# Mixture-of-experts kernel: the token lists by 9 wide products instead of 36 narrow ones, and low parts ahead of the routing's search

## The chip, the cores and the metric

The kernel runs on one core of one Trainium2 chip. The metric is the device time of one execution in microseconds (us). Engines: PE is TensorE, DVE VectorE, ACT ScalarE, POOL GpSimd, SP SyncE (which issues most DMAs).

## The reference

Pooled attention gives 4608 tokens of 512 features; the tokens then go to 8 experts of 576 tokens each. Logits of all tokens and experts are taken in descending order, and each token goes to the first expert of its own that still has room. Each expert is two matrix products with a ReLU between.

```python
logits = x @ w_gate                       # x: [4608, 512], 8 experts
order = np.argsort(-logits.flatten())
for idx in order:
    tok, e = int(idx) // E, int(idx) % E
    if assigned[tok] >= 0 or counts[e] >= cap:   # cap = 576
        continue
    assigned[tok] = e
    counts[e] += 1
for e in range(E):
    mask = assigned == e
    out[mask] = np.maximum(x[mask] @ w1[e], 0.0) @ w2[e]   # w1 512x1024, w2 1024x512
```

## The kernel before

**Attention** (to about 137 us) works on 36 tiles of 128 tokens, writes the tokens to `xd` in DRAM and keeps their logits in `lg`, 36 columns of 8 on 128 partitions.

**Routing** has 8 phases; each finds the next expert that fills up and the list of its tokens. A phase is a Python generator (`phase`, `search`, `close`), and its yields are the steps that a planner places. First the best remaining expert of each token (`best`), then four rounds of search for the threshold. A round compares (`cmp`, L598), counts by 9 products (L641, into `diagc` and `cnt`), sums by a fold (L652), tests (`g`, L659), and spreads the answer (L666). The first phase's rounds use narrow products (L603). `close` then makes the list: `own` marks the tokens, a scan and two products (L700, L701) number them (`si`), and each number is split into a low part of 5 bits and a block. `OHa` is a one-hot of the low part (L718), `OHb` a one-hot of the block times the token's column (L712) and, by ACT, times its partition (L713). 36 products, one for each column (L724), add both up: four groups of 32 partitions of PSUM for the columns modulo four, with 40 values. `cp` copies them out (L726), 8 products with `spread` (L732) bring the four groups together, and `rows` (L735) are the 576 token numbers as 5 columns of 128. Two products more (L750 and the counts around it) close the books. The step that yields "id" starts the DMA of the expert's w1, "rows" the gathers.

**Experts.** For each, POOL gathers the tokens' rows by five indirect DMAs (`xg`, L972); PE transposes each tile (L1004) into one of two PSUM banks `tp`; ACT copies out a rounded high part `xh`, and DVE takes the low part `xl`, what is left (L1008), which frees the bank. Weights are split likewise: `w1h` by ACT (L980), `w1l` by DVE (L984), eight pieces an expert; `w2h`, `w2l` (L990, L993). Stage 1 (L1028) adds three products of high and low parts, in blocks of 12 matmuls with 256 or 320 tokens; ACT writes `hh` and DVE the low part `hl` (L1036). Stage 2 (L1062, and L1067 for the last 64 rows) gives the output, which POOL scatters. The transposes of the next expert stand in stage 2, the last two sets in the next stage 1. The first expert takes w1 in two halves; a copy `late` (L1257), put behind an `xl` on DVE, makes the address of the second half, and another that of w2.

**What sets the order.** The order is written out as the program is built. Each engine does its list in order. `experts` keeps an estimated time `now`, moved by each PE matmul; `later` queues DVE work that is to be issued when its input should be there; `step` issues one step of the routing and estimates from its two numbers when DVE will be done (`ready`, `dve`). `advance` first issues queued work that is due, and then a routing step, unless its turn has not come. Between those, `Pieces` puts in parts of the weights. The line that decides is

```python
elif ready > now or waiting and turned[0] < 5 or not step(e):
```

so that the search goes ahead whenever its own last step should be done; only the first expert's transposes (`turned[0] < 5`) hold it, as long as anything is queued.

## Time and profile before

| | us |
|---|---|
| median of 3 runs | 629.12 |
| lowest, highest | 628.36, 630.3 |
| the profiled execution | 630.56 |
| its span, first to last instruction | 628.8 |
| mean granted TensorE clock | 0.986 |

In the profile a row of a view in order of time gives start, length, engine, line, operation, output<-inputs, shapes and count; in brackets stands how long the engine was idle before it and what released it. Rows of one line that follow each other are merged. Ends of matmuls are modelled and overlap, so the distance of starts is what one costs. A row of groups gives after the first bar the busy us and the mean ns of one, after the second the idle time before them.

### The profile page before, as it was taken

The page shows a single profiled execution, that of the slowest core. Times are in us where ns is not written, and L with a number is a line of the kernel's source. Part 1 is how long each engine was busy: PE and PEld are TensorE (multiplying, and loading weights), DVE is VectorE, ACT ScalarE, POOL GpSimd, SP SyncE. Part 2 cuts the span into 40 slices and gives each one's busy share as a digit, 9 for nine tenths or more (in the row PEclk, how much of TensorE's full clock was granted, in tenths as well). Part 3 has the DMA queues.
Part 4 walks back from the last instruction along what each step waited for, and adds up shares of the span by engine and source line. Part 5 has one row for each costly group of instructions (what it writes and reads, how often), then busy time and mean ns, then how long its engine had stood idle before and what let it go on. Part 6 is the DMA issues. An engine that isn't in the chain of part 4 may idle for free.

```text
span 628.8 us, 11882 instructions
## 1 busy us (share of the span) xinstructions
PE 602.0 (96%) x4543; PEld 521.4 (83%) x4543; DVE 391.4 (62%) x1142; ACT 242.9 (39%) x562; POOL 176.6 (28%) x218
## 2 busy tenths in 40 slices
PE   8999999985899999999999999999999999999994
PEld 6899999873797689769978987897799889879972
DVE  7587777887884778767862785386468326505300
ACT  7444444452451335233541433253336325514310
POOL 2999998001101410323011302120230113020021
PEclk9999999995999999999999999999999999999998
DMA  8999952222432543319003701640180046014011
GB/s 352 418 422 398 425 213 75 82 85 97 143 125 95 165 159 135 93 52 329 24 34 103 284 1 50 213 158 17 51 324 28 34 161 225 18 47 149 2 40 41
DMA packets 32611, 92.21 MB, mean 147 GB/s; under 512 B 3472, under 2 KB 3472, under 8 KB 29856
## 3 DMA queue, kind: packets, MB, share of 16 engines
q1 hardware_dynamic: 21296, 62.92, 26.7%
q0 software_dynamic: 5920, 18.95, 8.6%
q10 hardware_dynamic: 5328, 9.48, 4.0%
q8 instruction: 38, 0.62, 0.4%
q14 instruction: 29, 0.24, 0.1%
HBM read 72.46 MB, written 18.87 MB: 145 GB/s over the span
## 4 chain that ended last, share of the span: by engine, by line
PE 79%; issue 7%; DVE 5%; DMA 4%; POOL 3%; SPq 1%; ACT 1%; POOLq 0%; another core or an unknown queue 0%; ACTq 0%
PE h L1028 29%; PE h L1062 23%; PE psa L269 7%; PE pss L227 5%; PE h L1067 4%; PE tp L1004 2%; DMA rawk<-in_k_dram 2%; PE pse L256 2%; PE rt L256 1%; PE rt L724 1%; PE rt L641 1%; PE rt L217 1%; PE rt L603 1%; DMA out_dram<-yt,rows 1%; DMA raw<-in_moe_w_dram 1%
## 5 line engine op out<-in xcount | busy, mean ns | idle before, releaser
L1042 POOL DMA_INDIRECT out_dram<-yt,rows x29 | 30.6, 1056 | 264.3 <-ACT yt L1076 264.1
L1062 PE MATMUL h<-w2h,hl 128*128 128x512 f32 x256 | 102.6, 401 | 0.0
L1062 PE MATMUL h<-w2l,hh 128*128 128x512 f32 x256 | 102.0, 398 | 0.0
L1062 PE MATMUL h<-w2h,hh 128*128 128x512 f32 x256 | 101.1, 395 | 0.3 <-PEq L1126 0.3
L1028 PE MATMUL h<-xl,w1h 128*128 128x320 f32 (+1 forms) x512 | 95.1, 301 | 0.2 <-DVE late L1257 0.2
L1028 PE MATMUL h<-xh,w1l 128*128 128x320 f32 (+1 forms) x512 | 92.1, 298 | 0.5 <-DVE g L659 0.5
L1028 PE MATMUL h<-xh,w1h 128*128 128x320 f32 (+1 forms) x512 | 91.9, 300 | 0.3 <-issue 0.3
L1033 ACT ACTIVATE hh<-h 128x320 fp32r<-128x320 f32 (+1 forms) x128 | 52.0, 410 | 101.0 <-PE h L1028 97.9
L1028 PEld LDWEIGHTS h<-xh,w1h 128*128 128x128 f32 x512 | 75.6, 189 | 3.1 <-issue 3.1
L1028 PEld LDWEIGHTS h<-xl,w1h 128*128 128x128 f32 x512 | 76.8, 190 | 1.1 <-DVE late L1257 0.4
L1028 PEld LDWEIGHTS h<-xh,w1l 128*128 128x128 f32 x512 | 75.9, 189 | 0.9 <-DVE w1l L984 0.6
L972 POOL DMA_INDIRECT xg<-xd,rows x40 | 39.8, 995 | 125.4 <-DVE rows L735 69.1
L1008 DVE TENSOR_TENSOR xl<-tp,xh 128x512 fp32r<-128x512 f32 (+1 forms) x40 | 25.3, 633 | 78.4 <-ACT xh L1006 77.8
L1036 DVE SCALAR_TENSOR_TENSOR hl<-h,hh 128x320 fp32r<-128x320 f32 (+1 forms) x128 | 57.1, 451 | 26.6 <-ACT hr L1035 14.5
L1076 ACT ACTIVATE yt<-h 128x512 f32<-128x512 f32 x32 | 19.1, 597 | 123.8 <-PE h L1062 103.4
L269 PE MATMUL psa<-vblk,eT 128*128 128x146 f32 (+3 forms) x400 | 62.0, 302 | 0.0
L1062 PEld LDWEIGHTS h<-w2h,hh 128*128 128x128 f32 x256 | 48.2, 188 | 9.2 <-issue 0.7
L1062 PEld LDWEIGHTS h<-w2h,hl 128*128 128x128 f32 x256 | 48.3, 189 | 8.7
L1062 PEld LDWEIGHTS h<-w2l,hh 128*128 128x128 f32 x256 | 48.4, 189 | 8.2
L269 PEld LDWEIGHTS psa<-vblk,eT 128*128 128x128 f32 (+1 forms) x400 | 52.2, 180 | 1.7 <-POOL tk L172 0.3
L993 DVE TENSOR_TENSOR w2l<-raw,w2h 128x512 fp32r<-128x512 f32 x64 | 43.2, 681 | 3.7 <-ACT w2h L990 3.6
L984 DVE TENSOR_TENSOR w1l<-raw,w1h 128x512 fp32r<-128x512 f32 x64 | 41.2, 684 | 6.8 <-ACT w1h L980 6.4
(210 smaller groups left out, 907.9 us busy)
## 6 DMA issues: line engine op xcount, KB each, us to landing
raw<-in_moe_w_dram SPq DMA_DIRECT2D x64, 512.0 KB, 6.5
xd<-xt ACTq DMA_DIRECT2D x36, 256.0 KB, 3.9
rawv<-in_v_dram SPq DMA_DIRECT2D x7, 1280.0 KB, 8.4
rawk<-in_k_dram SPq DMA_DIRECT2D x7, 1152.0 KB, 11.6
rawq<-in_q_dram SPq DMA_DIRECT2D x7, 1152.0 KB, 13.3
rawk<-in_k_dram SPq DMA_DIRECT2D x2, 576.0 KB
rawv<-in_v_dram SPq DMA_DIRECT2D x1, 768.0 KB, 8.2
rawq<-in_q_dram SPq DMA_DIRECT2D x1, 640.0 KB, 9.1
```

Source lines behind the costliest of these rows:

```text
L227: nc.tensor.matmul(ps[cols, j // 2, 144 * (j % 2):144 * (j % 2) + 144], self.q_of(b, j, n, cols.stop - cols.start), self.kblk[b % 4][:, j] ...
L269: self.nc.tensor.matmul(o[h], self.eT[i][:, c, h], self.vblk[b % 4][:, self.BLOCKS[c]:self.BLOCKS[c + 1]], start=(c == cs[0]), stop=(c == ...
L972: nc.gpsimd.indirect_dma_start(out=self.xg[:n, t, :], out_offset=None, in_=self.xd, in_offset=bass.IndirectOffsetOnAxis(ap=rows[:n, t:t + ...
L984: self.nc.vector.tensor_tensor(l, raw, h.bitcast(F32), op=OP.subtract)
L993: self.nc.vector.tensor_tensor(self.w2l[:, i], self.raw2[e][:, i], self.w2h[:, i].bitcast(F32), op=OP.subtract)
L1008: later(1.3, 0.65, lambda: nc.vector.tensor_tensor(xl, ps[:, :, :n], xh, op=OP.subtract))
L1028: nc.tensor.matmul(ps[:, :m], a[:, j, fs], b[:, j, o], start=(n == 0), stop=(n == 11))
L1033: nc.scalar.activation(hh[:, f, o], ps[:, :m], AF.Relu)
L1036: later(0.65, 0.4, lambda f=f, o=o, m=m, ps=ps: nc.vector.scalar_tensor_tensor(hl[:, f, o], ps[:, :m], 0.0, hh[:, f, o].bitcast(F32), op0= ...
L1042: st = nc.gpsimd.indirect_dma_start(out=rows, out_offset=bass.IndirectOffsetOnAxis(ap=idx, axis=0), in_=y, in_offset=None)
L1062: nc.tensor.matmul(ps, a[:, f, o], b[:, f], start=(f == 0 and k == 0), stop=(f == 7 and k == 2))
L1067: nc.tensor.matmul(ps[64 * a:64 * a + 64, :256], self.hr[:, f], self.raw2[e][:, f, 256 * a:256 * a + 256], start=(f == 0), stop=(f == 7))
```

## The change

The list's 36 products become 9. Columns are regrouped so that product b holds the four columns b, b+9, b+18, b+27; the weights are 32 low parts times four columns, 128 in all, the moving side 20 blocks times four columns, 80. Of the 128x80 result only the entries count whose two column numbers agree: DVE multiplies with a 0/1 pattern `dq` and sums four, which leaves 20 values. One plane of float16 numbers is enough: `tokv` holds 1 + 128 b + partition, and the column's part, 0 to 3 times 1152, is put in afterwards (`qcol`) where the value is not zero. The products with `spread` add both; one is taken off at the end. ACT's pass with `pcol` is gone.

In the planner the low parts of x (`xl`) have a counter: while one is queued, no step of the routing is issued. The same holds while fewer than four low pieces of the next expert's w1 are issued, if its rows are found and its address is 9 us old. The old condition for the first expert goes.

```diff
 consts / more
+        self.tok = cst.tile([128, 9, 4], I32, name="tok")
+        nc.gpsimd.iota(self.tok, pattern=[[128, 9], [0, 4]], base=1, channel_multiplier=1)
...
-        self.colv = cst.tile([128, NC], BF, name="colv")
-        nc.vector.tensor_scalar(self.colv, t, 128.0, None, op0=OP.mult)
+        self.tokv = cst.tile([128, NC], F16, name="tokv")
+        nc.vector.tensor_copy(self.tokv, self.tok.rearrange("p b q -> p (b q)"))
...
-        self.OHb = cst.tile([128, 3, 20, NC], BF, name="OHb")
+        self.OHb = cst.tile([128, 2, 20, NC], F16, name="OHb")
...
 close
-        nc.vector.tensor_copy(sf, sab)
+        nc.vector.tensor_copy(sf.rearrange("p v (b q) -> p v b q", q=4), sab.rearrange("p v (q b) -> p v b q", q=4))
         OHb = self.OHb
         nc.vector.tensor_tensor(OHb[:, 0], sf[:, 1:2].to_broadcast([128, 20, NC]), self.blk, op=OP.is_equal)
-        nc.vector.tensor_tensor(OHb[:, 1], OHb[:, 0], self.colv[:, None].to_broadcast([128, 20, NC]), op=OP.mult)
-        nc.scalar.activation(OHb[:, 2], OHb[:, 0], AF.Copy, scale=self.pcol)
-        OHa = wk.tile([128, 32, NC], BF, name="OHa", bufs=1)
-        half = NC // 2
-        for cs in (slice(0, NC),) if k else (slice(0, half), slice(half, NC)):
-            n = cs.stop - cs.start
-            nc.vector.tensor_tensor(OHa[:, :, cs], sf[:, 0:1, cs].to_broadcast([128, 32, n]), self.j16[:, :, cs],
-                                    op=OP.is_equal)
+        nc.vector.tensor_tensor(OHb[:, 1], OHb[:, 0], self.tokv[:, None].to_broadcast([128, 20, NC]), op=OP.mult)
+        OHa = wk.tile([128, 9, 32, 4], F16, name="OHa", bufs=1)
+        nc.vector.tensor_tensor(OHa, sf[:, 0].rearrange("p (b q) -> p b q", q=4)[:, :, None].to_broadcast([128, 9, 32, 4]),
+                                self.j16[:, None, :, :4].to_broadcast([128, 9, 32, 4]), op=OP.is_equal)
         yield 2.6, 2.6
         ps = self.psum()
-        for c in range(NC):
-            q = slice(32 * (c % 4), 32 * (c % 4) + 32)
-            nc.tensor.matmul(ps[q, :40], OHa[:, :, c], OHb[:, 1:3, :, c], start=(c < 4), stop=(c >= NC - 4))
-        cp = wk.tile([128, 40], BF, name="cp")
-        nc.vector.tensor_copy(cp, ps[:, :40])
-        yield 0.25, 0.25
+        for b in range(9):
+            nc.tensor.matmul(ps[:, :80], OHa[:, b].rearrange("p a q -> p (a q)"), OHb[:, 1, :, 4 * b:4 * b + 4],
+                             start=(b == 0), stop=(b == 8))
+        own = wk.tile([128, 20, 4], F32, name="rowd")
+        nc.vector.tensor_tensor(own, ps[:, :80].rearrange("p (k q) -> p k q", q=4),
+                                self.dq[:, None, :].to_broadcast([128, 20, 4]), op=OP.mult)
+        cp = wk.tile([128, 2, 20], F16, name="cp")
+        nc.vector.tensor_reduce(cp[:, 0], own, axis=AX.X, op=OP.add)
+        nc.vector.tensor_scalar(cp[:, 1], cp[:, 0], 0.0, self.qcol, op0=OP.is_gt, op1=OP.mult)
+        yield 0.6, 0.6
...
-        nc.vector.tensor_copy(rows, ps[:, :5])
+        nc.vector.tensor_scalar(rows, ps[:, :5], -1.0, 0.0, op0=OP.add, op1=OP.max)
...
 experts
-            elif ready > now or waiting and turned[0] < 5 or not step(e):
+            elif ready > now or first(e) or not step(e):
                 break
...
+    def first(e):
+        if lows:
+            return True
+        return e in toks and e in pieces and pieces[e].l < 4 and due(e, "id", 9)
...
-        X.xt(t, name, bufs, later)
+        X.xt(t, name, bufs, later_low)     # counts lows up when queued, down when issued
```

Three places of DVE's list show what moves. The first is in expert 0, where the third and later sets of transposes are split; `fold` to `oh` are the start of the routing's second phase, `cmp` its first comparison, `late` the copy that starts a weight load. Before:

```order
L584 RECIPROCAL scale<-steps 128x1
L1036 SCALAR_TENSOR_TENSOR hl<-h,hh 128x256
L1008 TENSOR_TENSOR xl<-tp,xh 128x4x128
L1257 COPY late<-eid 1x1
L1008 TENSOR_TENSOR xl<-tp,xh 128x4x128
L1036 SCALAR_TENSOR_TENSOR hl<-h,hh 128x256
L502 TENSOR_SCALAR td<-jp 128x4
```

and now, in the new file's line numbers:

```order
L596 RECIPROCAL scale<-steps 128x1
L518 MEMSET fold 128x64
L520 TENSOR_REDUCE fold<-ident 128x32
L558 TENSOR_REDUCE bv_258<-lg 128x36
L570 TENSOR_SCALAR q_2147<-bv_258,lo_255,scale 128x36
L576 TENSOR_SCALAR q32c<-q_2147 128x36
L563 CAST q16a<-q32c 128x36
L564 TENSOR_TENSOR oh_260<-lg,bv_258 128x288
L1051 SCALAR_TENSOR_TENSOR hl<-h,hh 128x256
L1023 TENSOR_TENSOR xl<-tp,xh 128x4x128
L1291 COPY late<-eid 1x1
```

The choice of best experts has come ahead of `hl`, `xl` and `late`; behind these, the last two `xl` now stand ahead of `cmp`.

The second place is the end of expert 0's stage 2, where the second expert's transposes are split and the third phase of the routing begins. Before:

```order
L775 TENSOR_TENSOR lg<-lg,pen_2790 128x288
L580 TENSOR_SCALAR width<-hi,lo_249 128x1
L582 TENSOR_SCALAR steps<-shares,width 128x4
L584 RECIPROCAL scale<-steps 128x1
L984 TENSOR_TENSOR w1l<-raw_2642,w1h 128x512
L546 TENSOR_REDUCE bv_251<-lg 128x36
L558 TENSOR_SCALAR q_2824<-bv_251,lo_249,scale 128x36
L564 TENSOR_SCALAR q32c<-q_2824 128x36
L551 CAST q16a<-q32c 128x36
L552 TENSOR_TENSOR oh_253<-lg,bv_251 128x288
L598 TENSOR_TENSOR cmp<-q16a,j_190 128x1152
L1008 TENSOR_TENSOR xl<-tp,xh 128x4x128
```

Now:

```order
L790 TENSOR_TENSOR lg<-lg,pen_2768 128x288
L1023 TENSOR_TENSOR xl<-tp,xh 128x4x128
L999 TENSOR_TENSOR w1l<-raw_2619,w1h 128x512
L1023 TENSOR_TENSOR xl<-tp,xh 128x4x128
L999 TENSOR_TENSOR w1l<-raw_2619,w1h 128x512
L1023 TENSOR_TENSOR xl<-tp,xh 128x4x128
L592 TENSOR_SCALAR width<-hi,lo_255 128x1
```

All three `xl` have come ahead of the search. On PE a fourth set of transposes stands in this stage 2, where there were three.

The third place is the token list as it stands in the later experts, here the last list. Before:

```order
L718 TENSOR_TENSOR OHa<-sf,j_190 128x1152
L1008 TENSOR_TENSOR xl<-tp,xh 128x4x64
L1036 SCALAR_TENSOR_TENSOR hl<-h,hh 128x256 x2
L726 CAST cp<-rt 128x40
L1036 SCALAR_TENSOR_TENSOR hl<-h,hh 128x256
L735 CAST rows<-rt 128x5
```

Now:

```order
L727 TENSOR_TENSOR OHa<-sf,j_196 128x1152
L1051 SCALAR_TENSOR_TENSOR hl<-h,hh 128x256 x3
L736 TENSOR_TENSOR rowd<-rt,dq 128x80
L740 TENSOR_REDUCE cp<-rowd 128x20
L741 TENSOR_SCALAR cp<-cp,qcol 128x20
L1051 SCALAR_TENSOR_TENSOR hl<-h,hh 128x256
L750 TENSOR_SCALAR rows<-rt 128x5
```

The last `xl` has gone ahead of the list, and three `hl` stand between OHa and the three new operations. On PE, 25 stage-1 matmuls are now between the numbering products and the list's (27 before) and 13 between the list's and those with `spread` (12 before).

More of the change, by code (lines that the diff above doesn't have):

```diff
@@ L429, in first @@
         nc.gpsimd.iota(self.ti, pattern=[[1, 36]], base=0, channel_multiplier=0)
+        self.tok = cst.tile([128, 9, 4], I32, name="tok")
+        nc.gpsimd.iota(self.tok, pattern=[[128, 9], [0, 4]], base=1, channel_multiplier=1)
+        self.p4 = cst.tile([128, 32], I32, name="p4")
+        nc.gpsimd.iota(self.p4, pattern=[[-4, 32]], base=0, channel_multiplier=1)
+        self.pq = cst.tile([128, 1], I32, name="pq")
+        nc.gpsimd.iota(self.pq, pattern=[[0, 1]], base=0, channel_multiplier=1)
     def consts(self, jp, ident):
@@ L466, in more @@
         t = cst.tile([128, 32], I32, name="tf")
-        nc.vector.tensor_scalar(t, jp[:, :32], 31, None, op0=OP.bitwise_and)
-        self.spread = cst.tile([128, 224], BF, name="spread")
+        nc.vector.tensor_scalar(t, self.p4, -4, None, op0=OP.bitwise_and)
+        self.spread = cst.tile([128, 224], F16, name="spread")
         nc.vector.memset(self.spread, 0.0)
@@ L484, in more @@
         self.ohs = [cst.tile([128, NC, 8], BF, name=f"oh{i}") for i in range(2)]
-        self.OHb = cst.tile([128, 3, 20, NC], BF, name="OHb")
+        self.OHb = cst.tile([128, 2, 20, NC], F16, name="OHb")
+        t = cst.tile([128, 4], I32, name="td")
+        nc.vector.tensor_scalar(t, jp[:, :4], 3, None, op0=OP.bitwise_and)
+        self.dq = cst.tile([128, 4], F32, name="dq")
+        nc.vector.tensor_scalar(self.dq, t, 0.0, None, op0=OP.is_equal)
+        t = cst.tile([128, 1], I32, name="tq")
+        nc.vector.tensor_scalar(t, self.pq, 3, None, op0=OP.bitwise_and)
+        self.qcol = cst.tile([128, 1], F32, name="qcol")
+        nc.vector.tensor_scalar(self.qcol, t, 1152.0, None, op0=OP.mult)
     def psum(self):
@@ L644, in search @@
                 own = wk.tile([128, 8, 4], F32, name="diagc")
-                nc.vector.tensor_tensor(own, ps[:, :32].rearrange("p (c e) -> p e c", c=4), self.diag, op=OP.mult)
+                nc.vector.tensor_tensor(own, ps[:, :32].rearrange("p (c e) -> p e c", c=4), self.dq[:, None, :].to_broadcast([128, 8, 4]),
+                                        op=OP.mult)
                 cnt = wk.tile([128, 8], F16, name="cnt")
@@ L726, in close @@
-        nc.vector.tensor_copy(cp, ps[:, :40])
-        yield 0.25, 0.25
-        cpv = cp.rearrange("p (v j g) -> p v j g", v=2, g=4)
+        for b in range(9):
[4 more added lines that the diff above has]
+                                self.dq[:, None, :].to_broadcast([128, 20, 4]), op=OP.mult)
@@ L729, in close @@
+        cp = wk.tile([128, 2, 20], F16, name="cp")
+        with nc.allow_low_precision(reason="one number up to 1152 and zeros"):
+            nc.vector.tensor_reduce(cp[:, 0], own, axis=AX.X, op=OP.add)
+        nc.vector.tensor_scalar(cp[:, 1], cp[:, 0], 0.0, self.qcol, op0=OP.is_gt, op1=OP.mult)
+        yield 0.6, 0.6
+        cpv = cp.rearrange("p v (j g) -> p v j g", g=4)
         ps = self.psum()
@@ L734, in close @@
         rows = wk.tile([128, 5], I32, name="rows", bufs=3)
-        nc.vector.tensor_copy(rows, ps[:, :5])
+        nc.vector.tensor_scalar(rows, ps[:, :5], -1.0, 0.0, op0=OP.add, op1=OP.max)
         self.rows = rows
         halves = wk.tile([128, 1], I32, name="halves", bufs=3)
-        nc.vector.scalar_tensor_tensor(halves, ps[:, 4:5], 2.0, self.upper, op0=OP.mult, op1=OP.add)
+        nc.vector.scalar_tensor_tensor(halves, rows[:, 4:5], 2.0, self.upper, op0=OP.mult, op1=OP.add)
         self.halves = halves
@@ L1145, in experts @@
     held, waiting = [], []
+    lows = 0
     now, dve, ready = 0.0, 0.0, 0.0
@@ L1224, in by, with later_low, g @@
                 self.next()
+    def later_low(after, t, f):
+        nonlocal lows
+        def g():
+            nonlocal lows
+            lows -= 1
+            f()
+        lows += 1
+        later(after, t, g)
+    def first(e):
+        if lows:
+            return True
+        return e in toks and e in pieces and pieces[e].l < 4 and due(e, "id", 9)
     def turn(e, t, name="tp", bufs=2):
```

4 lines of the change are left out of this document (removed).

## Prediction

> **What bounds the kernel now.** First the page's busy times and its chain of waits, to see which engine the end hangs on.
>
> ```profile
> span 628.8 us, 11882 instructions
> PE 602.0 (96%) x4543; PEld 521.4 (83%) x4543; DVE 391.4 (62%) x1142; ACT 242.9 (39%) x562; POOL 176.6 (28%) x218
> PE 79%; issue 7%; DVE 5%; DMA 4%; POOL 3%; SPq 1%; ACT 1%; POOLq 0%; another core or an unknown queue 0%; ACTq 0%
> ```
>
> TensorE is busy 96% of the span and holds 79% of the chain. So PE's queue is the clock: a matmul taken out of it in the expert stage is time saved, and work on DVE counts only where PE waits for it. Then stretches of one expert each, from its first stage-1 matmul to the next expert's.
>
> ```profile
> 161.00:224.00 63.00, 61.04 (x463) 51.01 (x463) 45.45 (x145) 23.89 (x55) 10.42 (x14) 1.00 0.38 125
> 398.20:455.70 57.50, 57.50 (x433) 49.44 (x431) 36.48 (x113) 21.58 (x51) 10.68 (x15) 1.00 0.32 115
> 511.10:566.40 55.30, 55.23 (x389) 48.78 (x387) 24.03 (x56) 21.36 (x51) 10.61 (x15) 1.00 0.33 120
> ```
>
> The columns after the length are PE, PEld, DVE, ACT and POOL. From the middle on PE has no idle time at all; in the first stretch it idles 2 us. What is left to gain late is thus the length of PE's own list, and waits are to be had early only. The clock column is 1.00 in all three, so no change of clock enters.
>
> **The products of the token list.** Once for each expert, 36 products of 32 weight columns (L724) become 9 of 128. Their price is read where they sit in PE's queue, beside the nearest thing to the new ones: the search's 9 products with 128 weight columns and 32 moving ones (L641).
>
> ```profile
> 517.02 0.64 PE L1028 MATMUL h<-xh,w1l 128*128 128x256 f32 x4
> 517.50 0.40 PE L1028 MATMUL h<-xl,w1h 128*128 128x256 f32 x2
> 517.83 0.92 PE L724 MATMUL rt<-OHb,OHa 128*32 128x40 bf16 x36
> 518.67 0.51 PE L1028 MATMUL h<-xl,w1h 128*128 128x256 f32 x2
> ...
> 437.82 0.39 PE L1062 MATMUL h<-w2h,hh 128*128 128x512 f32 x1
> 438.05 0.39 PE L641 MATMUL rt<-oh,cmp 128*128 128x32 bf16 x9
> 438.29 0.48 PE L1062 MATMUL h<-w2h,hl 128*128 128x512 f32 x1
> ```
>
> Starts are what counts, since ends overlap. Four 256-column matmuls take 517.50 - 517.02 = 0.48, so two end at 517.74; the next stage-1 matmul starts at 518.67. The 36 products cost 0.93 us, of which 0.09 is lost ahead of them, about 0.18 behind. The 9 of L641 cost 438.29 - 438.05 = 0.24, or 25 to 27 ns each, with nothing lost around them. The new ones move 80 columns. Below: 25 ns, as 32 columns take, 0.23 in all. Above, far: a 256-column float32 matmul takes 120 ns, 1.08 in all, a loss of 0.15. Between: 512 columns take 0.23 us, 0.44 ns a column, so 80 take 35 ns; that row and L641 lie on one line to within 10 ns, so I take 35 to 40, 0.35 in all. Saved 0.58 for each of the seven lists that stand among expert matmuls: **-4.1 us** (-4.9 to +1.1).
>
> One rule speaks against this. The Trainium skill, TensorEngine Tiling (Array Packing), section Theoretical Speedup, gives a product of at most 32 weight columns a fourfold rate when four share the array, and the old products are laid out so. Then 36 of 40 columns would take as long as 9 of 40, some 0.16 us, and 9 of 80 twice that. By this trace they do not: the group's 0.92 less one 0.26 of a product is 0.66 us from first to last start, 18 ns for 40 columns, 0.46 ns a column, the single-file rate. By the rule the saving would be the 0.27 around the products less 0.19, about 0.6 us in seven lists.
>
> **The first list** stands alone: nothing is there to hide it, and the first expert waits.
>
> ```profile
> 151.51 0.82 DVE L718 TENSOR_TENSOR OHa<-sf,j 128x576 bf16<-128x576 f16 x2
> 152.02 0.96 PE L724 MATMUL rt<-OHb,OHa 128*32 128x40 bf16 x36 [2.40 <-DVE OHa L718]
> 153.02 0.20 DVE L726 CAST cp<-rt 128x40 bf16<-128x40 f32 x1 [0.68 <-PE rt L724]
> 153.66 0.17 DVE L735 CAST rows<-rt 128x5 int32<-128x5 f32 x1 [0.44 <-PE rt L732]
> 154.71 0.98 POOL L972 DMA_INDIRECT xg<-xd,rows  x1 [46.52 <-DMA raw<-in_moe_w_dram]
> 161.07 0.74 PE L1028 MATMUL h<-xh,w1h 128*128 128x256 f32 x4 [0.26 <-issue]
> L218 DVE TENSOR_TENSOR vblk<-rt,mask 128x88 f32<-128x88 f32 x7 | 1.7, 246 | 2.3 <-PE rt L217 2.3
> L648 DVE TENSOR_REDUCE cnt<-diagc 128x8 f16<-128x32 f32 x24 | 4.5, 187 | 0.8
> L675 DVE TENSOR_SCALAR sel<-q,up 128x36 bf16<-128x36 f16 x7 | 1.6, 228 | 0.0
> ```
>
> Before, the products start when half of OHa is there and end at 152.98, 0.65 after all of it. Now OHa is one operation of the same 1152 elements, and 9 products follow: at the rate of the 36 in this place (0.96 - 0.26 over 1440 columns, 0.5 ns) 0.36 to start and 0.26 to drain the last, no gain against 0.65. Then the copy `cp` of 0.20 becomes three operations: a product of 128x80 out of PSUM (0.24, like 128x88), a sum (0.22, over 0.187 for 32 elements) and a scalar operation (0.22): 0.68 and two steps between, +0.5. The ACT pass with `pcol` (0.90) leaves, but it lay beside DVE's 0.82 and sets nothing. POOL's gather follows `rows`, and PE's first matmul the gather: **+0.6 us** (0.2 to 1.0). If the gather really waits for the weights that the row names, up to 0.9 of it is cover and the term is near nothing.
>
> In the other seven lists the three operations stand behind three `hl` of about 0.4 each:
>
> ```profile
> 516.54 0.75 DVE L718 TENSOR_TENSOR OHa<-sf,j 128x1152 bf16<-128x1152 f16 x1
> 518.79 0.20 DVE L726 CAST cp<-rt 128x40 bf16<-128x40 f32 x1 [0.50 <-PE rt L724]
> 520.22 0.36 PE L732 MATMUL rt<-cp,spread 128*128 128x5 bf16 x8
> ```
>
> PE reaches the next 8 products (L732) 0.35 + 13 x 0.12 = 1.9 us after the first of the 9. DVE needs 1.2 + 0.7 = 1.9 after OHa, which was ready 517.83 - 517.29 = 0.5 before PE asked; two matmuls fewer stand between now, so some 0.3. I put this at nothing, with little cover to spare; each 0.1 us that it lacks costs 0.7 in all.
>
> **The order of DVE's work.** PE's real waits among experts, from PE's rows in time:
>
> ```profile
> 203.77 0.39 PE L1062 MATMUL h<-w2h,hh 128*128 128x512 f32 x1
> 204.71 0.35 PE L732 MATMUL rt<-cp,spread 128*128 128x5 bf16 x8 [0.55 <-DVE cp L726]
> 213.55 0.40 PE L1062 MATMUL h<-w2h,hh 128*128 128x512 f32 x1
> 214.81 0.66 PE L1004 MATMUL tp<-ident,xg 128*128 128x128 f32 x4 [0.86 <-DVE xl L1008]
> 223.53 0.18 PE L652 MATMUL rt<-cnt,fold 128*128 128x8 f16 x1
> 224.23 0.38 PE L1028 MATMUL h<-xh,w1l 128*128 128x256 f32 x1 [0.52 <-DVE g L659]
> 303.74 0.31 PE L1028 MATMUL h<-xh,w1h 128*128 128x320 f32 x1
> 304.55 0.39 PE L641 MATMUL rt<-oh,cmp 128*128 128x32 bf16 x9 [0.50 <-DVE cmp L598]
> ```
>
> Less a 0.23 matmul the first two lose 0.71 and 1.03; the third loses 0.66 (a small product takes 0.04), the last, less 0.15, another 0.66: 3.1 us together. The 1.03 is what the change names: the fourth set of transposes needs a PSUM bank that `xl` frees, and DVE is in the search:
>
> ```profile
> 211.70 0.45 DVE L546 TENSOR_REDUCE bv<-lg 128x36 f32<-128x288 f32 x1
> 213.40 0.75 DVE L598 TENSOR_TENSOR cmp<-q16a,j 128x1152 bf16<-128x1152 f16 x1
> 214.07 0.68 DVE L1008 TENSOR_TENSOR xl<-tp,xh 128x512 fp32r<-128x512 f32 x1
> 163.02 0.16 DVE L584 RECIPROCAL scale<-steps 128x1 f32<-128x1 f32 x1
> 166.88 0.11 DVE L506 MEMSET fold<- 128x64 uint32 x1
> 168.72 0.75 DVE L598 TENSOR_TENSOR cmp<-q16a,j 128x1152 bf16<-128x1152 f16 x1
> ```
>
> With `xl` and the first four `w1l` ahead of the search, the waits at 213 and 223 should go; but two updates of `lg` and four `w1l` still stand ahead of the first `xl`, so I leave 0.6 there. The wait at 203 has five matmuls of cover now instead of three (0.46 more), against three operations instead of one (0.5): half of it stays. Of 0.71 + 1.03 + 0.66 = 2.4, **-1.5** (0 to -2.4). At 304 the search comes three stage-1 matmuls (0.44) later in PE's queue: **-0.5** (0 to -0.66).
>
> Against it: in expert 0, `fold` and the choice of best experts (166.88 to 168.72, 1.84 us) now run at 163.2, ahead of the third `xl`. That `xl` frees the bank for the fifth transposes and is followed by the copy `late` that starts the second half of w1. PE should wait some 0.3 us there; the weights come about 1.5 later, which the 48 matmuls of 320 columns (7 us) cover. Two more small products fall among the last rows' matmuls, where one costs some 0.2 us. Together **+0.3** (0 to 1.0).
>
> The constants on POOL and DVE (three iotas, four small operations at 10 us) lie beside the first K load and cost nothing.
>
> **Sum**: -4.1 + 0.6 - 1.5 - 0.5 + 0.3 = -5.2 us. The profiled execution took 630.56 us around its span of 628.8, 1.4 over the median of the runs; taken off the median, 629.12 - 5.2 = **623.9 us**.
>
> **Rivals.** (a) Only the products help: each PE wait removed comes back at the next operation of the search, which is held, not shortened. For it: DVE has more to do in each list, and the first stretch has 45 of 63 us on DVE. Against it: in the late ones it is 24 to 36 of 55 to 57. -4.1 + 0.6 + 0.6 for new waits: 626.2. (b) All four waits go, none is added, and a product takes 25 ns: -4.9 + 0.2 - 2.4 - 0.7 = -7.8, 621.3. For it: the waits are all DVE's order; against it: something is always ahead of the first `xl`. (c) Nine wide products cost what 36 narrow ones did: the time is the rest of the sum, 628.0. For it: I have no row of 80 columns; against it L641. The tiling rule's 0.6 us belongs here too, 627.4. (d) Slower: PE waits at L732 in all seven lists, because the three operations stand behind an `hl` whose ACT half is itself late. Over 0.75 us each this eats the whole gain; at 1.0 us, -5.2 + 7.0: 630.9. For it: cover is just used up; against it: `cp` was done 520.22 - 518.99 = 1.2 us early, and 0.5 of that is spent now.
>
> **Chances**: forecast 0.50 (622 to 626 by its own terms), (a) 0.22, (b) 0.15, (c) 0.07, (d) 0.06. The measurement tells 0.3%, 1.9 us, from no change. Faster: 0.50 + 0.15 + 0.17 of (a) = 0.82; same: 0.05 of (a) + 0.07 = 0.12; slower 0.06. The range 620.5 to 628.0 takes in (a), (b) and (c), 0.8 below (b) because single runs lie 0.8 us under the median, and leaves out (d).
>
> **What would show it.** The new L733 group starts within 0.35 us and the next expert matmul follows at once, in all seven lists; late stretches are 0.6 us shorter each. `rows` of the first list comes 0.6 later, and so does PE's first stage-1 matmul. No wait on `xl` of over 0.6 in the first boundary, none at 223. I am wrong if the L732 products wait for `cp`, if PE idles at the fifth transposes of expert 0 for over 0.6 us, or if 9 products take over 0.5 us.

## The result, and the profile after

The changed kernel takes 624.06 us (five runs, 624.02 to 624.17) against 629.22 us (five runs, 628.36 to 631.07) on the same chip: 0.992 of the time before, 95% interval 0.9907 to 0.9933. 623.9 had been forecast, in a range of 620.5 to 628.0. The profiled execution took 624.06 us around a span of 622.2.

The page of the changed kernel: span, busy times and chain.

```profile
span 622.2 us, 11468 instructions
PE 597.3 (96%) x4327; PEld 518.6 (83%) x4327; DVE 396.9 (64%) x1159; ACT 238.3 (38%) x554; POOL 180.1 (29%) x221
PE 83%; issue 7%; DVE 4%; DMA 2%; ACT 1%; POOL 1%; another core or an unknown queue 0%; POOLq 0%; ACTq 0%
```

TensorE (PE) is still the bound, with 216 products fewer (8 lists of 27); VectorE (DVE) has 5.5 us more work and a smaller share of the chain. Then single experts' stretches; the columns after the length are PE, PEld, DVE, ACT and POOL.

```profile
161.00:219.50 58.50, 58.25 (x418) 49.60 (x418) 44.73 (x139) 22.91 (x53) 9.95 (x14) 1.00 0.40 135
219.50:279.40 59.90, 59.31 (x440) 49.87 (x438) 44.44 (x145) 21.61 (x51) 10.81 (x15) 1.00 0.33 110
505.10:559.90 54.80, 54.74 (x362) 48.45 (x360) 24.64 (x58) 20.91 (x50) 10.88 (x15) 1.00 0.34 121
```

In the first expert's stretch PE idles 0.25 us now instead of 2; in the second's still 0.6. Measured exactly, from one expert's first stage-1 matmul to the next one's (for the eighth, to the start of its own last matmul), in us. A second profile of each kernel, taken later, stands below its first; the other rows are the experiments.

| kernel | first stage-1 matmul at | 0 | 1 | 2 | 3 | 4 | 5 | 6 | 7 | sum |
|---|---|---|---|---|---|---|---|---|---|---|
| before | 161.07 | 61.55 | 59.98 | 58.00 | 57.57 | 57.55 | 55.37 | 55.36 | 52.73 | 458.1 |
| before, again | 162.39 | 61.52 | 59.99 | 58.03 | 57.51 | 57.53 | 55.35 | 55.37 | 52.73 | 458.0 |
| changed | 161.05 | 58.49 | 59.83 | 57.04 | 56.94 | 56.91 | 54.85 | 54.82 | 52.72 | 451.6 |
| changed, again | 162.25 | 58.40 | 59.83 | 57.05 | 56.94 | 56.91 | 54.85 | 54.83 | 52.76 | 451.6 |
| e1, list alone | 161.02 | 59.14 | 59.70 | 56.73 | 57.62 | 57.61 | 54.75 | 54.74 | 52.72 | 453.0 |
| e2, order alone | 161.93 | 60.11 | 59.42 | 58.04 | 57.79 | 57.87 | 55.47 | 55.45 | 52.72 | 456.9 |
| e3, 36 narrow products | 160.93 | 58.88 | 60.06 | 57.27 | 57.14 | 57.17 | 55.05 | 55.07 | 52.72 | 453.4 |
| e4, earlier high parts | 161.00 | 58.50 | 59.06 | 57.04 | 56.94 | 56.91 | 54.84 | 54.83 | 52.73 | 450.9 |
| e5, e4 + narrow first list | 161.27 | 58.45 | 59.05 | 57.02 | 56.92 | 56.91 | 54.81 | 54.81 | 52.72 | 450.7 |
| e6, e4 + no search in the tail | 161.56 | 57.91 | 57.94 | 57.70 | 56.94 | 56.91 | 54.84 | 54.82 | 52.72 | 449.8 |
| e7, cover taken away | 161.07 | 59.39 | 60.08 | 57.63 | 57.51 | 57.50 | 55.40 | 55.39 | 52.72 | 455.6 |
| f1, e5 + e6, constants moved | 161.03 | 58.19 | 57.97 | 58.64 | 56.92 | 56.91 | 54.83 | 54.81 | 52.72 | 451.0 |
| f2, f1 + both holds, wider turns | 160.44 | 58.48 | 59.29 | 57.72 | 56.91 | 56.90 | 54.55 | 54.53 | 52.73 | 451.1 |
| g1, e6 + wider turns at the end | 161.05 | 57.96 | 57.95 | 57.94 | 56.94 | 56.91 | 54.57 | 54.55 | 52.72 | 449.5 |

Two profiles of one kernel agree in these stretches to 0.1 us, though their first matmul lies 1.2 to 1.3 us apart. So the stretches, not single times, tell what an edit does among the experts; the eight of them shrank by 6.5 us.

**The list in its place**, in the last stretch that has one; above on PE, below on DVE.

```profile
512.57 0.40 PE L1043 MATMUL h<-xh,w1l 128*128 128x256 f32 x2
512.81 0.51 PE L733 MATMUL rt<-OHb,OHa 128*128 128x80 f16 x9
513.15 0.48 PE L1043 MATMUL h<-xh,w1l 128*128 128x256 f32 x2
...
514.79 0.36 PE L747 MATMUL rt<-cp,spread 128*128 128x5 f16 x8
```

```profile
513.47 0.23 DVE L736 TENSOR_TENSOR rowd<-rt,dq 128x80 f32<-128x80 f32 x1
513.73 0.24 DVE L740 TENSOR_REDUCE cp<-rowd 128x20 f16<-128x80 f32 x1
514.01 0.23 DVE L741 TENSOR_SCALAR cp<-cp,qcol 128x20 f16<-128x20 f16 x1
```

The nine start 0.24 after two 256-column matmuls, so nothing is lost ahead of them, and the next matmul starts 0.34 after their first. Behind them 0.08 is lost: the next two matmuls take 0.32 (513.47 - 513.15) instead of 0.24. Behind the old kernel's 36 the same two took 0.35. The eight small ones come 0.55 after the last of the three operations (514.79 - 514.24): PE does not wait for them, in any of the seven lists.

**The first list**, before and then changed (PE to the first stage-1 matmul, and DVE's `rows`).

```profile
149.46 0.16 PE L701 MATMUL rt<-inc,tri 128*128 128x1 bf16 x1 [0.73 <-DVE eid L693]
```

```profile
148.86 0.16 PE L714 MATMUL rt<-inc,tri 128*128 128x1 bf16 x1 [0.73 <-DVE eid L706]
151.75 0.78 PE L733 MATMUL rt<-OHb,OHa 128*128 128x80 f16 x9 [2.72 <-DVE OHa L727]
153.13 0.59 PE L747 MATMUL rt<-cp,spread 128*128 128x5 f16 x8 [0.61 <-DVE cp L740]
153.76 0.17 DVE L750 TENSOR_SCALAR rows<-rt 128x5 int32<-128x5 f32 x1 [0.42 <-PE rt L747]
161.05 0.73 PE L1043 MATMUL h<-xh,w1h 128*128 128x256 f32 x4 [0.26 <-ACT xh L1021]
```

From the last small product ahead of the list to the start of `rows`: 153.66 - 149.46 = 4.20 before, 4.90 now, 0.7 more. Some 0.5 of this is the three operations. The other 0.2 is the products, which end 0.84 after `OHa` instead of 0.65: TensorE's granted clock is 0.50 here (the column behind POOL's), and the nine start 67 ns apart instead of 38. First this place, then the last list:

```profile
151.70:152.60 0.90, 0.78 (x9) 0.59 (x9) 0.04 (x1) 0.00 (x0) 0.00 (x0) 0.50 0.81 205
512.80:513.20 0.40, 0.40 (x12) 0.39 (x10) 0.40 (x3) 0.00 (x0) 0.00 (x0) 1.00 1.04 398
```

Yet the first stage-1 matmul came no later, because this execution reached the place 0.6 earlier. That 0.6 lies at 22 us, where the old kernel's PE waited for `rawq` (first fence) and the changed one's didn't (second).

```profile
22.25 1.17 PE L227 MATMUL pss<-kblk,rawq 128*64 128x144 f32 x14 [0.43 <-DMA rawq<-in_q_dram]
```

```profile
21.32 1.45 PE L227 MATMUL pss<-kblk,rawq 128*64 128x144 f32 x16
```

**The waits among experts.** Those at 204, 214 and 224 us are gone: the fourth set of transposes at the first boundary comes with the others and waits for nothing (first line). A new wait stands in the second expert: PE starts two matmuls and is then held for the search's nine products, because DVE has `cmp` late.

```profile
211.69 0.60 PE L1019 MATMUL tp<-ident,xg 128*128 128x128 f32 x4
...
232.43 0.40 PE L1043 MATMUL h<-xh,w1l 128*128 128x256 f32 x2
233.43 0.39 PE L653 MATMUL rt<-oh,cmp 128*128 128x32 bf16 x9 [0.59 <-DVE cmp L610]
```

```profile
231.53 0.69 DVE L1008 TENSOR_TENSOR w2l<-raw,w2h 128x512 fp32r<-128x512 f32 x1 [1.35 <-ACT w2h L1005]
232.14 0.16 DVE L681 TENSOR_REDUCE up<-rt 128x1 f32<-128x8 f32 x1
232.33 0.24 DVE L684 TENSOR_SCALAR q<-q32c,up 128x36 f16<-128x36 f32 x1
232.61 0.76 DVE L610 TENSOR_TENSOR cmp<-q,j 128x1152 bf16<-128x1152 f16 x1
```

The search's next step (`up`, then `q`, then `cmp`) is queued on DVE behind a low part of w2, and that low part stood 1.35 us waiting for its own high part on ScalarE (ACT). 233.43 - 232.43 less two matmuls of 0.12 is 0.76 us.

### The profile page after: what moved, and what is told of

Read it like the earlier page. It is cut to its first block, busy times and chain, and to the rows that moved or that the text cites. A ratio compares the mean times of both kernels' runs of the same rounds, so it can differ in the third digit from the quotient of the medians.

```text
span 622.2 us, 11468 instructions
## 1 busy us (share of the span) xinstructions
PE 597.3 (96%) x4327; PEld 518.6 (83%) x4327; DVE 396.9 (64%) x1159; ACT 238.3 (38%) x554; POOL 180.1 (29%) x221
## 4 chain that ended last, share of the span: by engine, by line
PE 83%; issue 7%; DVE 4%; DMA 2%; ACT 1%; POOL 1%; another core or an unknown queue 0%; POOLq 0%; ACTq 0%
PE h L1043 30%; PE h L1077 25%; PE psa L269 8%; PE pss L227 6%; PE h L1082 4%; PE tp L1019 2%; PE pse L256 2%; PE rt L256 1%; PE rt L653 1%; PE rt L217 1%; PE rt L615 1%; DMA rawk<-in_k_dram 1%; DMA out_dram<-yt,rows 1%; PE rt L208 1%; DMA xg<-xd,rows 1%
## 5 line engine op out<-in xcount | busy, mean ns | idle before, releaser
L1077 PE MATMUL h<-w2h,hh 128*128 128x512 f32 x256 | 102.5, 400 | 0.3 <-PEq L1141 0.3
L1077 PE MATMUL h<-w2h,hl 128*128 128x512 f32 x256 | 101.0, 395 | 0.0
L1043 PE MATMUL h<-xh,w1l 128*128 128x320 f32 (+1 forms) x512 | 95.4, 301 | 0.0
L1043 PE MATMUL h<-xl,w1h 128*128 128x320 f32 (+1 forms) x512 | 92.8, 300 | 0.0
L987 POOL DMA_INDIRECT xg<-xd,rows x40 | 42.3, 1056 | 131.8 <-DVE rows L750 48.6
L1043 PEld LDWEIGHTS h<-xh,w1l 128*128 128x128 f32 x512 | 77.2, 189 | 0.5
```

The source lines that it names most:

```text
L987: nc.gpsimd.indirect_dma_start(out=self.xg[:n, t, :], out_offset=None, in_=self.xd, in_offset=bass.IndirectOffsetOnAxis(ap=rows[:n, t:t + ...
L1043: nc.tensor.matmul(ps[:, :m], a[:, j, fs], b[:, j, o], start=(n == 0), stop=(n == 11))
L1077: nc.tensor.matmul(ps, a[:, f, o], b[:, f], start=(f == 0 and k == 0), stop=(f == 7 and k == 2))
```

## Experiments

Each set ran on one chip; the old kernel's median on it is named, since it went from 628.7 to 631.3 us between chips, while the changed kernel gave 624.06 and 624.05 on two.

### e1 and e2: each half alone

e1 keeps the list and takes the new hold out:

```diff
-            elif ready > now or first(e) or not step(e):
+            elif ready > now or waiting and turned[0] < 5 or not step(e):
...
-        X.xt(t, name, bufs, later_low)
+        X.xt(t, name, bufs, later)
```

e2 is the old kernel with `later_low` and `first(e)` put in at the same two places.

> The new token list alone; the planner's hold of the search steps is the old one. Theory A, the terms add up one by one: seven lists at 0.53 us less each (-3.7), the first list +0.7 where nothing hides it, and the waits of the first boundary (on xl at about 213 us, 1.0; behind the search at about 223, 0.7) stay as they were: 629.2 - 3.7 + 0.7 = 626.2 us, 625.4 to 627.0, with expert 0's stretch at 60 to 61.5 us. Theory B, the list carries the whole change and the order nothing: 624.1 us, with expert 0's stretch near 58.5.

> The new hold alone: low parts of x and of the first four pieces of w1 ahead of search steps, with the old list of 36 products. Theory A: the first boundary's waits go (-2.4), the one at 304 (-0.7) and one at 258 (-0.3) too, and a new one of 0.75 on cmp near 232 comes with three search products among the 64-row matmuls (+0.5): -2.2, so 627.0 us, 626.2 to 628.0. The lists keep 0.93 us of TensorE each. Theory B: the waits only move to the next step of the search, 628.7 to 629.7 us.

e1: 625.96 us (625.82 to 626.58), e2: 629.11 (628.74 to 631.35), the old kernel 630.8 beside them; ratios 0.9931 (0.9915 to 0.9947) and 0.998 (0.9969 to 0.9991). e1 lies inside theory A's range. e2 is 1.1 above its own range and inside theory B's, though on a chip that is itself slower for the old kernel; it is 1.7 below that kernel instead of 2.2. In the stretches: list alone -5.1, order alone -1.2, both -6.5, so they nearly add up (e1's runs took 2.2 us beyond their span, the others 1.8, so its time shows some 0.4 less than its stretches). For e1 theory B falls: the list carries most, but not all. For e2 it is half right. The first two stretches became 2.0 shorter, so the order's part is real; but those of experts 3 to 6 grew by 0.7 together, and in the first one PE waits some 0.7 us for `cmp` at 219.5, where neither the old nor the changed kernel does. Part of what the order alone removes comes back at the search.

But theory A's detail for e1 was wrong. Its first stretch is 59.1, not 60 to 61.5. The waits at 204 and 224 went with the list alone (they are gone in e2 as well); only the one for `xl` stayed, and later ones grew or came new. PE in e1:

```profile
213.03 0.66 PE L1019 MATMUL tp<-ident,xg 128*128 128x128 f32 x4 [0.51 <-DVE xl L1023]
...
258.05 0.66 PE L1019 MATMUL tp<-ident,xg 128*128 128x128 f32 x4 [0.93 <-DVE xl L1023]
...
375.86 0.39 PE L653 MATMUL rt<-oh,cmp 128*128 128x32 bf16 x9 [0.65 <-DVE cmp L610]
```

And on DVE, what stood ahead of `xl` and of that `cmp`:

```profile
256.64 0.75 DVE L610 TENSOR_TENSOR cmp<-q16a,j 128x1152 bf16<-128x1152 f16 x1
257.31 1.28 DVE L1023 TENSOR_TENSOR xl<-tp,xh 128x512 fp32r<-128x512 f32 x2
...
373.97 0.69 DVE L999 TENSOR_TENSOR w1l<-raw,w1h 128x512 fp32r<-128x512 f32 x1 [1.78 <-ACT w1h L995]
```

With the search let in ahead of `xl`, PE waits at both boundaries (0.68 and 1.10 us over its matmul); with the hold both are gone. The wait at 376 (0.81 us, and one of 0.85 at 433) is of the kind at 232: a low part stuck behind its own high part, the search behind it. The changed kernel has neither. A wait for the search is thus no fixed item that an edit removes or leaves: every edit shifts the planner's clock, and the steps land elsewhere.

### e3: 36 narrow products with one number plane

```diff
-        for b in range(9):
-            nc.tensor.matmul(ps[:, :80], OHa[:, b]..., OHb[:, 1, :, 4 * b:4 * b + 4], ...)
-        own = ...; nc.vector.tensor_tensor(own, ps[:, :80]..., self.dq...)
-            nc.vector.tensor_reduce(cp[:, 0], own, axis=AX.X, op=OP.add)
+        for c in range(NC):
+            q = slice(32 * (c % 4), 32 * (c % 4) + 32)
+            nc.tensor.matmul(ps[q, :20], OHa[:, c // 4, :, c % 4], OHb[:, 1, :, c], ...)
+        nc.vector.tensor_copy(cp[:, 0], ps[:, :20])
```

> One float16 number plane as in the changed kernel, but 36 products of 32 weight columns and 20 moving ones (the fold over four columns is then not needed; one operation less on VectorE). Theory rate: a narrow product costs its columns one after the other, 0.46 ns each, 9 ns for 20: 0.33 + 0.27 around the group = 0.60 us a list, 0.26 more than the nine: 624.1 + 1.8 = 625.9 us, less up to 0.3 in the first list. Theory fixed price: a product costs about 18 ns however few columns it moves: 0.93 us a list, 624.1 + 4.1 = 628.2 us. Theory of four narrow products side by side: 0.08 + 0.27 = 0.35 us a list, 624.1 us or a little less.

625.85 us (625.37 to 626.37), where 625.9 was expected of the rate. PE in the last list:

```profile
513.96 0.40 PE L1039 MATMUL h<-xh,w1l 128*128 128x256 f32 x2
514.29 0.56 PE L734 MATMUL rt<-OHb,OHa 128*32 128x20 f16 x36
514.78 0.50 PE L1039 MATMUL h<-xh,w1l 128*128 128x256 f32 x2
```

The group is 0.56 long; less the 0.2 that the last product takes to drain (a single small one is listed with 0.16 to 0.19) the 36 start within some 0.36 us, 10 ns each for 20 columns, where 40 columns took 18 to 20. The fixed price of 18 ns is out. But the price by the column does not mean one after the other. Seen through a window of a few hundredths of a microsecond, the groups of the last list begin like this, in the old kernel up to 517.90 and in e3 up to 514.33:

```profile
517.83 0.28 PE L724 MATMUL rt<-OHb,OHa 128*32 128x40 bf16 x4
514.29 0.22 PE L734 MATMUL rt<-OHb,OHa 128*32 128x20 f16 x4
```

Four products, one for each quarter of PSUM's partitions, start within 10 ns of each other, and the next four 80 ns later with 40 columns, 41 ns later with 20. So four do start side by side, but a set of four takes as long as four in a row at 0.5 ns a column. A rate four times as high is not there (the Trainium skill, TensorEngine Tiling (Array Packing), section Theoretical Speedup, has up to fourfold). Nor do the sets follow the clock: in the first list, at a granted clock of 0.50, they come 79 and 41 ns apart, while the nine wide ones go from 38 to 67. What sets their pace is not shown. In all these kernels the moving side of a narrow product takes every 36th number, and no run tries it otherwise.

Each list costs 0.2 to 0.25 us more than the nine wide ones. The first list, though, was 0.55 shorter, 4.35 from the small product to `rows` instead of 4.90: 0.23 of it because the narrow group is 0.55 long at that clock and the wide one 0.78, the rest because one operation fewer stands behind it:

```profile
149.38 0.16 PE L714 MATMUL rt<-inc,tri 128*128 128x1 bf16 x1 [0.73 <-DVE eid L706]
153.73 0.17 DVE L746 TENSOR_SCALAR rows<-rt 128x5 int32<-128x5 f32 x1 [0.42 <-PE rt L743]
```

### e4: high parts of w2 earlier

```diff
+            if e and n == 54:
+                w2.up()
+                w2.up()
             if n >= 64 and n % 2:
                 w2.by((n - 70) // 14 if n > 70 else 0)
```

> The changed kernel with the first two high parts of w2 of experts 1 to 7 (ScalarE) ten matmuls earlier, so that the first low part on VectorE doesn't wait for its own high part. Theory A: TensorE's wait of 0.75 us on cmp near 232 us is VectorE standing 1.4 us behind that low part with the search's next step queued after it; it shrinks to 0.2 or less: 623.4 us, 623.1 to 623.7. Theory B: the search step is late for its own chain of operations, the wait stays: 624.0 to 624.2 us. If the weights have not landed by then, ScalarE stalls and the hidden layer's parts come late: above 624.4 us.

623.25 us (623.13 to 624.37). Only ACT's order is changed; expert 1's stretch fell from 59.83 to 59.06, and no other one moved by more than 0.02. PE at the same place:

```profile
232.38 0.40 PE L1043 MATMUL h<-xh,w1l 128*128 128x256 f32 x2
232.62 0.39 PE L653 MATMUL rt<-oh,cmp 128*128 128x32 bf16 x9
```

The wait of 0.76 us is gone, and so is DVE's of 1.35 ahead of that low part. The cause was thus the low part waiting at the head of DVE's queue. This is shown, theory B is out.

### e7: the cover behind the list taken away

```diff
         nc.vector.tensor_tensor(own, ps[:, :80]..., self.dq...)
+        for _ in range(4 if k else 0):
+            nc.vector.tensor_tensor(own, own, self.dq[:, None, :].to_broadcast([128, 20, 4]), op=OP.mult)
```

> The changed kernel with four more operations of 128x80 (about 0.23 us each, 0.9 together) between the nine products and the second eight, in lists 2 to 8. The eight products now have 0.54 us to spare after the sum's last operation. Theory A: cover of 0.54 goes first, the rest is TensorE's wait at each of the seven: 0.2 to 0.4 us each, 624.1 + 1.4 to 2.8 = 625.5 to 626.9 us. Theory B: lists on VectorE are off the path and cost nothing: 624.0 to 624.4 us. Theory C: each operation counts in full: 624.1 + 7 x 0.9 = 630.4 us.

628.11 us (627.96 to 629.26) beside 624.05 of the changed kernel on its chip, +4.1. First DVE, then PE:

```profile
517.21 1.07 DVE L739 TENSOR_TENSOR rowd<-rowd,dq 128x80 f32<-128x80 f32 x4
```

```profile
517.90 0.52 PE L1045 MATMUL h<-xh,w1l 128*128 128x256 f32 x3
518.61 0.58 PE L749 MATMUL rt<-cp,spread 128*128 128x5 f16 x8 [0.19 <-DVE cp L742]
```

Theory A's mechanism, with its size off: operations that depend on each other start 0.27 us apart, not 0.23, so 1.1 us were added to the sum. 0.5 of it is cover, and the other 0.55 to 0.6 is PE's in each of the stretches 2 to 6 (0.9 in the first, 0.25 in the second). In the kernel as changed, half a microsecond is all that keeps the three new operations free.

### e5, e6 and the last versions

The changed kernel ran unaltered in the set of e5, e6 and e7:

> The changed kernel once more, unaltered, so that the three others of this set have it on their own chip: 623.9 to 624.4 us; TensorE's wait on cmp near 232 us (0.75 over its matmul) is there again if it is a matter of the order, and the wait for rawq at 22 us, which only the first profile of the old kernel had, may come or not.

624.05 us (623.89 to 625.26) beside 628.74 of the old kernel. The wait on `cmp` is there again, 0.75 us at 233.7, so it belongs to the order; no wait for `rawq`.

e5 adds e3's narrow products to e4, in the first list alone, with five more constants for them (0.1 to 0.2 us each on DVE at 9 to 10 us):

```diff
+        spread, qcol = (self.spread, self.qcol) if k else (self.spread0, self.qcol0)
+        if k:
             ... nine wide products and the fold, as changed
+        else:
+            ... 36 narrow products and one copy, as in e3
```

> The first list alone with 36 products of 32 weight columns and 20 moving ones (no fold behind it), the other seven with the nine wide ones; and the earlier high parts of w2. Theory A: the first list sets when the gather and the first stage-1 matmul start; from the last small product ahead of it to rows it took 5.07 us with nine wide products and 4.52 with the narrow ones, so 0.55 us less than with the earlier high parts alone: 622.7 us (622.4 to 623.0). Theory B: the gather waits for something else there (it starts 0.88 us after rows, 0.27 in the other seven lists), and nothing is gained: 623.2 us.

623.23 us (623.12 to 623.36), 0.8 below the changed kernel on its chip, and that is e4's share: nothing came of the first list. The list itself was as short as in e3, but the first stage-1 matmul came at 161.27 instead of e4's 161.00. The gather followed `rows` by 0.88 us as in the others, so theory B's reason is not it. DVE reached its first softmax at 11.13 us in e5, at 9.96 in the changed kernel; 0.5 of this is a K transfer that came later in that execution, the rest the five constants:

```profile
11.13 0.75 DVE L237 TENSOR_REDUCE mx<-pss 128x8 f32<-128x576 f32 x1
```

e6 is e4 with the search held between the 64-row matmuls that end an expert's second stage (64 tokens are left; in the rows they are 128*64, 64 weight columns):

```diff
-            elif ready > now or first(e) or not step(e):
+            elif ready > now or hold or first(e) or not step(e):
...
-            advance(min(e + 1, 7), dt)
+            advance(min(e + 1, 7), dt, 96 <= n < 103)
```

> The earlier high parts of w2, and no search step issued between the 64-row matmuls that end an expert. Theory A: each small product between them costs 0.20 us to come out of and some 0.15 to go back, five of them in the first two experts; beside stage-1 matmuls they cost 0.03 each: 0.5 to 0.8 us less than with the earlier high parts alone, 622.6 us (622.3 to 622.9). Theory B: the search's later steps fall at other places, and a new wait for VectorE takes the gain or more: 623.2 to 624.2 us, with a wait of over 0.4 us in expert 1's or 2's stretch that was not there.

622.30 us (622.07 to 622.75), 0.989 of the old kernel on its chip (0.987 to 0.9911), 1.75 below the changed one. The changed kernel's PE, where two search products break the row, and where nothing does:

```profile
215.20 2.38 PE L1082 MATMUL h<-raw,hr 128*64 128x256 f32 x20
217.51 0.39 PE L653 MATMUL rt<-oh,cmp 128*128 128x32 bf16 x9
217.83 1.08 PE L1082 MATMUL h<-raw,hr 128*64 128x256 f32 x8
218.84 0.18 PE L665 MATMUL rt<-cnt,fold 128*128 128x8 f16 x1
219.54 0.50 PE L1043 MATMUL h<-xh,w1h 128*128 128x256 f32 x2
...
501.50 3.67 PE L1082 MATMUL h<-raw,hr 128*64 128x256 f32 x32
505.11 0.74 PE L1043 MATMUL h<-xh,w1h 128*128 128x256 f32 x4
```

Unbroken, the 32 take 505.11 - 501.50 = 3.61 us; broken twice, 219.54 - 215.20 = 4.34. The nine products' own 0.24 and the single one's 0.04 leave 0.45, so 0.22 us for each break. Theory A, and more than it asked: -0.6 and -1.1 in the first two stretches, of which +0.7 comes back in the third, where the postponed steps run. No wait as in theory B came up in these three.

f1 joins e5 and e6 and moves the constants: what the first list needs into DVE's waits in the first search, the rest into expert 0. f2 adds the old hold to the new one in expert 0 and sets the transposes 1.65 us apart instead of 1.4. The old kernel ran once more beside them.

```diff
-            sh = self.wanted()
+            sh = self.wanted()
+            if k < 2:
+                sh = chain(sh, self.wide() if k else self.narrow())
```

```diff
-            elif ready > now or hold or first(e) or not step(e):
+            elif ready > now or hold or waiting and turned[0] < 5 or first(e) or not step(e):
...
-        if t < upto and due(e, "rows", 6.5 + 1.3 * t) and now >= last + 1.4:
+        if t < upto and due(e, "rows", 6.5 + 1.3 * t) and now >= last + 1.65:
```

> The old kernel once more, unaltered, for a second profile of it. Theory A: two waits of the first profile belong to that execution and not to the kernel, the 0.64 us that TensorE lost at 22 us for rawq and the 0.71 at 204 us, where its wait for cp ended 1.1 us after cp had; without them the profiled execution is near 629.2 us, and expert 0's stretch 60.8 instead of 61.55. Theory B: both are there again, the stretch is 61.5.

> Narrow products in the first list alone, the earlier high parts of w2, no search step between the 64-row matmuls, and the constants moved: none more than in the old kernel stand on VectorE ahead of the first softmax (the two that the first list needs go into waits of the first search, the rest into expert 0). Theory A: with the narrow products in the first list alone, nothing was gained because five more constants pushed the first softmax back by 0.7 us; without them the first list's 0.55 us is there, and some 0.2 more from the four constants of the changed kernel that leave: 622.3 - 0.55 to 0.9 = 621.4 to 621.8 us. Theory B: the start of the experts hangs on something else, 622.1 to 622.5 us.

> The same, and both holds of the search steps in expert 0, the old one and the new one, with the turns of transposes 1.65 us apart instead of 1.4. Theory A: the fifth transposes of expert 0 wait 0.34 us because the choice of best experts stands ahead of the xl that frees their bank; that wait goes, and so do 0.2 us at the third transposes of experts 6 and 7: 0.5 to 0.8 us under the kernel before it in this set. Theory B: the search, 1.5 us later, meets other work in the first two experts and loses as much or more in a wait that was not there: -0.2 to +0.8 us against it.

Theory A fell in all three. f1: 622.90 us (622.83 to 623.46), above theory B's range too, f2: 622.86 (622.20 to 623.31), the old kernel 630.83 on this chip. In f1 the first softmax is back at 9.94 us, and the first stage-1 matmul still at 161.03: PE, earlier at 22 us, now waits there for `rawq`, as the old kernel did.

```profile
22.29 1.17 PE L228 MATMUL pss<-kblk,rawq 128*64 128x144 f32 x14 [0.52 <-DMA rawq<-in_q_dram]
...
309.93 0.66 PE L1046 MATMUL tp<-ident,xg 128*128 128x128 f32 x4 [0.71 <-DVE xl L1050]
```

So the shift by five constants was real in e5, but here the earlier start met a transfer that wasn't there yet. Whether it is there goes with the execution: the changed kernel reached this place at 21.32 us, f1 at 21.30, and only f1 waited; e6, with the changed kernel's constants, came at 21.19 and waited 0.61. The second row is a wait that expert 2 got in return, with other constants in its search. In f2 the wait at expert 0's fifth transposes went, and waits of 0.73 us at 211 us and of 0.43 and 0.44 in expert 1 came: theory B. Only the wider turns did what they should, -0.28 in each of the stretches 5 and 6.

The second profile of the old kernel (631.81 us): both waits are there again, and expert 0's stretch is 61.52.

g1 takes e6 and that one piece of f2, for the last two experts:

```diff
-        ... and now >= last + 1.4:
+        ... and now >= last + (1.65 if e > 5 else 1.4):
```

> The earlier high parts of w2, no search step between the 64-row matmuls, and, for the last two experts alone, the turns of transposes 1.65 us apart instead of 1.4. Theory A: the third transposes of experts 6 and 7 wait one 0.23 us matmul for the xl that frees their bank; one matmul more between the turns covers that, and the stretches of experts 5 and 6 go from 54.84 and 54.82 us to 54.6: 622.3 - 0.5 = 621.8 us. Theory B: the wait moves to the next set of transposes, the stretches stay and so does the time, 622.1 to 622.7 us.

622.61 us (621.72 to 623.18) beside 631.25 of the old kernel, 0.9863 (0.9843 to 0.9882). The stretches 5 and 6 fell by 0.27 each, as theory A has it, and expert 2's is 0.24 longer, so half of the gain went elsewhere; the time itself lies in theory B's range. By the sum of the stretches g1 is the shortest, 449.5 us against 449.8 of e6 and 451.6 of the change; by the times, on different chips, which of e6 and g1 is faster is not settled. Both beat the change, e6 on the same chip, g1 by its stretches.

## Why the prediction held, and where its steps did not

The time was forecast within 0.2 us, and there is luck in that: two misses of 0.7 us cancel. In the eight stretches the forecast had -4.1 - 1.5 - 0.5 + 0.3 = -5.8, and they fell by 6.5. Ahead of the experts it had +0.6. The two profiled executions show no loss there, but the medians do. Behind the start of the last expert's last matmul both profiles have the same 9.6 us, and both runs took 1.8 us beyond their span. With these, the old kernel's median of 629.22 us puts its first stage-1 matmul near 159.7 us, 1.3 earlier than the changed kernel's 161.05. This is an estimate: it takes the stretches of a median run to be those of the two profiles. Then -6.5 + 1.3 = -5.2, as the medians have it. Of the 1.3 the first list is 0.7; what the rest is stays open.

So the step that took the sum off the median is not shown right. It takes the changed kernel's profiled execution to lie as far above its median as the old kernel's, 1.4 us; but both profiles of the old kernel caught runs above the median, and the changed kernel's first profile is its median run.

1. **Seven lists, -4.1.** The mechanism was right, the price too: 0.34 us for nine products (0.35 forecast), 38 ns each. "Nothing lost around them" was misread: 0.08 is lost behind them, as behind other groups of small products (behind the 9 of L641 the next matmul took 438.61 - 438.29 = 0.32 instead of 0.23), and 0.11 behind the 36. So a list in its place saves 0.61. The late stretches, which hold nothing else that changed, fell by 0.52 and 0.54, so -3.7 in all; the missing 0.08 went to the two numbering products, which had stood right behind a set of transposes and now stand alone among stage-1 matmuls. Rival (c), nine wide products as dear as 36 narrow ones, is out. The reading "the single-file rate" of the narrow ones does not hold either: they start in fours (e3). The price taken for them was measured and stays.
2. **First list, +0.6.** +0.7 measured in the list, 0.2 of it in a term put at nothing: the nine start 67 ns apart where the sum took 40. "No change of clock enters" is right for the three stretches it names; the first list stands at 0.50. The gather follows `rows` by 0.88 us in every kernel here, so the doubt whether it waited for weights is settled: no cover there. That the first stage-1 matmul of the profile came no later was luck of the `rawq` wait at 22 us, of which the prediction knew nothing. Nor are the constants free on DVE: with K there at 4.88 us, the changed kernel starts its first softmax at 9.96; f2, which moves them, at 9.42 with K at 4.80. But f2 then waited for `rawq`, so no run shows what they cost in time.
3. **Three waits, -1.5 of 2.4.** All 2.4 went. The step that failed is "half of it stays" at 204 and 0.6 left at 214. Either half of the change alone removes 204 and 224, and the hold the one for `xl`. Why DVE's copy at 204 came 1.2 us after the products in both profiles of the old kernel, and in no other, stays open. The first stretch fell by 3.06; the list and the waits at 204 and 214 are 2.3 of this, and 0.3 is a round of nine search products that now falls into the second stretch. The rest is not accounted for.
4. **Wait at 304, -0.5.** It went whole, -0.66, in e1 too; and -0.30 at 258 that the prediction did not count.
5. **New waits, +0.3.** This term was mis-sized most. The fifth transposes of expert 0 wait 0.34 us, as forecast, but another wait of 0.35 nearby left. The 0.76 at 232 was not foreseen. Of search products between the 64-row matmuls there are three more than before, at 0.22 us for each break; the prediction named two at 0.2, and its own parts, 0.3 and twice 0.2, make 0.7 and not 0.3. Together some +1.4, above its range of 0 to 1.0. Of the rivals, (a) was thus half right in its mechanism, a removed wait that comes back at a later operation of the search, and (b) in that all four waits went. e4 shows the cause of the dearest, and it was not the load on DVE but one instruction waiting at its head.

(d), slower through the three operations: PE had 0.55 us to spare where 0.3 was forecast. e7 took it away and shows the stated price, 0.7 us in all for each 0.1 that the cover lacks: 0.55 beyond it took back 4.1 of the 5.2 gained.

## What to carry to other kernels

Where an in-order engine feeds the bound, look first at what waits at the head of its queue: a cheap operation that stands behind one still waiting for another engine waits with it, and moving the other engine's work ten matmuls earlier was worth 0.8 us here. Price small products from rows of their own shape, with what is lost behind the group, and at the clock of the place; keep them out of a row of matmuls with another tile shape. Compare stretch by stretch: an edit that shifts a planned order moves waits about, so its total is known only from a run.
